# Loading feed-forward weights in fp32 through one hardware queue, with the casts on GpSimd, in a fused scan and feed-forward kernel

## The chip, the core and the metric

The kernel runs on one core of a Trainium2 chip. The metric is the device time of one execution in microseconds. A core has TensorE (PE in the profile, with its weight loads as PEld), VectorE (DVE), ScalarE (ACT), GpSimd (POOL) and SyncE (SP), and 16 DMA engines that move data between HBM and the on-chip SBUF. Matmuls write into PSUM, [...]. Each engine runs its own instructions in order, and semaphores tie the engines together.

## The reference

The first half is a chunked linear recurrence over 4 batches, 8 heads and 768 time steps, with head dimension 32 and state dimension 16. Its result, as 3072 tokens of 256 features, goes through a feed-forward layer with a squared ReLU.

```python
cum = np.cumsum(la, axis=-1)                       # la = log of the decay a
L = np.exp(cum[..., :, None] - cum[..., None, :]) * causal
y_intra = ((Cc @ Bc^T) * L) @ xc
y_inter = (Cc @ state) * np.exp(cum)[..., None]
state   = decay_full * state + sum_j decay_from_j * Bc_j xc_j^T
...
h   = np.maximum(x @ w_in, 0.0)                    # (3072, 256) @ (256, 2048)
out = h * h @ w_out                                # (3072, 2048) @ (2048, 256)
```

All inputs and the output are fp32; w_in and w_out are 2 MB each.

## The kernel before, in words

The work is cut into twelve units: batch b of 4 and a stretch of 256 time steps j of 3. Unit k is batch k % 4, stretch k // 4 (`UNITS`). Partition t of a unit holds two neighbouring time steps. The decays are carried by a cumulative product of a (`P_sb` and its reciprocal `Pinv`), with which C and B are scaled.

What happens to a unit: `ph_load` (L124) loads C, B and x in fp32. `prep_c` (L164), `prep_b` (L172) and `prep_x` (L183) scale and cast them to bf16 into `jt` and `xs`. `ph_tr` (L202) transposes `jt` into `bct`, on PE for the first five units and with a DMA transpose for the others. `ph_mt` (L234) makes the score matrices in PSUM banks 0 to 3; `ph_mask` (L256) applies the causal mask on DVE and writes them as bf16 `mts`, either straight from PSUM or from a bf16 copy `raw` that `ph_raw` (L251) made on ACT. `ph_yu` (L263) makes the outputs y of a unit ("Y") from `mts`, `xs` and the carried state `Sd`, copied into `T`, and the state products U of a unit ("U") from `xs` and `jt`. `ph_s` (L336) folds U into the state z, and GpSimd spreads z into the bf16 operand `Sd` (L357).

The feed-forward part of unit b has eight steps fp of 256 hidden features. `mm1` (L371, in the schedule "u") multiplies T by w_in, and ACT applies the ReLU (L380); `square` (L383, "s") squares on DVE; `mm2` (L389, "d") multiplies by w_out and accumulates. In the schedule u13 is mm1 of unit 1 at step 3.

The order is written by hand. Up to the word `first` (L542) it is the plain sequence of calls; `first` then lists the steps of units 0 and 1, with the third unit's preparation, masks and products between them; after it a table by step number (`at`) drives units 2 to 11, one mm1 and one mm2 per step. PE passes the list strictly in order.

The weights are in bf16 in SBUF, in four tiles for each matrix. `load_w_in` (L149) and `load_w_out` (L153) are DMAs issued by GpSimd that cast from fp32 on the way. They stand between GpSimd's other instructions: w_in block 0 before the first unit is prepared, then w_out 0 in two parts, w_in 1, w_out 1, w_in 2, then the third unit (C and B in fp32, x cast on the way by `load_x`, L141), then w_out 2, w_in 3, w_out 3. Two tiny casts into `spare` (L452, L508) hold GpSimd back until a result of another engine is there. The second one, with three one-element memsets into the load buffers (L131), holds the loads of units 3 to 5 back until a mask of the third unit is done. The other loads are issued by SyncE.

Of the kernel before, what the change touches and what calls it, by code (L numbers as in the profile page):

```python
# [10 lines left out]
FP32 = mybir.dt.float32  # L11
BF16 = mybir.dt.bfloat16
# [11 lines left out]
def _dap(base: bass.AP, offset_elems: int, dims):  # L24

    return bass.AP(tensor=base.tensor, offset=base.offset + offset_elems,
                   ap=[list(d) for d in dims])
# [3 lines left out]
def kernel(  # L31
# [15 lines left out]
    NU = 12  # L47
# [36 lines left out]
    pick_p = const.tile([96, 2, 12], FP32, name="pick_p")  # L84
    P_sb = const.tile([128, 2, 96], FP32, name="P_sb")
    Pinv = const.tile([128, 2, 96], FP32, name="Pinv")
    spare = const.tile([128, 1], FP32, name="spare")
    Ptot = const.tile([128, 2, 12], FP32, name="Ptot")


# [1 line left out]

    idle = const.tile([128, 128], BF16, name="idle")

    w_in_b = [wpool.tile([128, 2, 512], BF16, name=f"w_in_b{i}") for i in range(4)]
    w_out_b = [wpool.tile([128, 4, 256], BF16, name=f"w_out_b{i}") for i in range(4)]
    QP = const.tile([128, 12, 2, 4], FP32, name="QP")

    pp = psum.tile([128, 8, 512], FP32, name="pp")
# [21 lines left out]

    loaded, live = {}, {}

    def ph_load(k, order="CBx", eng=None, gate=False):  # L124
        b, j = UNITS[k]
        t = loaded.setdefault(k, {})
        for what in order:
            src, w = {"B": (B, N), "C": (C, N), "x": (x, D)}[what]
            dst = nat.tile([128, NH, 2 * w], FP32, tag=f"{what}_nat", name=f"{what}_nat{k}")
            if gate:  # L130
                nc.gpsimd.memset(dst[:, 0, 0:1], 0.0)  # L131
            parts = 2 if k == NU - 1 and what == "B" else 1
            for p in range(parts):
                hs = NH // parts
                (eng or nc.sync).dma_start(  # L135
                    out=dst[:, p * hs:(p + 1) * hs],
                    in_=_dap(src, (b * NH * S + p * hs * S + j * 256) * w,
                             [[2 * w, 128], [S * w, hs], [1, 2 * w]]))
            t[what] = dst

    def load_x(k):  # L141

        b, j = UNITS[k]
        xs = const.tile([128, NH, 2 * D], BF16, name=f"xb{k}")
        nc.gpsimd.dma_start(out=xs, in_=_dap(x, (b * NH * S + j * 256) * D,
                                             [[2 * D, 128], [S * D, NH], [1, 2 * D]]))
        live.setdefault(k, {})["xs"] = xs

    def load_w_in(i):  # L149
        nc.gpsimd.dma_start(  # L150
            out=w_in_b[i], in_=_dap(moe_w_in, i * 512, [[2048, 128], [128 * 2048, 2], [1, 512]]))

    def load_w_out(i, parts=1):  # L153
        n = 4 // parts
        for p in range(parts):
            nc.gpsimd.dma_start(  # L156
                out=w_out_b[i][:, p * n:(p + 1) * n],
                in_=_dap(moe_w_out, (i * 4 + p * n) * 128 * 256, [[256, 128], [128 * 256, n], [1, 256]]))

    def idle_products(n):  # L160
        for _ in range(n):
# [10 lines left out]
    def prep_b(k, eng):  # L172
        b, j = UNITS[k]
        for g in range(2):
            o = _fap(jt[k % 3], 16 * g, [[384, 2], [32, 4], [1, 16]])
            i = _fap(loaded[k]["B"], 128 * g, [[16, 2], [32, 4], [1, 16]])
            if k == 0:
                eng.copy(out=o, in_=i)
            else:
                eng.tensor_tensor(out=o, in0=i, in1=_fap(Pinv, b * 24 + 12 * g + j, [[96, 2], [3, 4], [0, 16]]),  # L180
                                  op=ALU.mult)

    def prep_x(k, eng):  # L183

        xs = prep.tile([128, NH, 2 * D], BF16, tag="xs", name=f"xs{k}")
        if k == 0:
            eng.tensor_tensor(
                out=_fap(xs, 0, [[64, 8], [32, 2], [1, 32]]),
                in0=_fap(loaded[k]["x"], 0, [[64, 8], [32, 2], [1, 32]]),
                in1=_fap(Pinv, 0, [[3, 8], [96, 2], [0, 32]]), op=ALU.mult)  # L190
        else:
            eng.tensor_copy(out=xs, in_=loaded[k]["x"])  # L192
        live.setdefault(k, {})["xs"] = xs
# [62 lines left out]
    def ph_mask(k, q):  # L256
        t = raw_scores.pop((k, q), None)
        nc.vector.tensor_tensor(  # L258
            out=live[k]["mts"][:, q],
            in0=(pp[:, q, :] if t is None else t).rearrange("p (r g i) -> p r g i", r=2, g=2),  # L260
            in1=_fap(mask, 0, [[128, 2], [0, 2], [1, 128]]), op=ALU.mult)
# [108 lines left out]

    def mm1(blk, fp, edge):  # L371
        h = bank(edge)
        wb, wo = fp // 2, 2 * (fp % 2)
        for i in range(2):
            for g in range(2):
                nc.tensor.matmul(pp[:, h, i * 256:(i + 1) * 256], w_in_b[wb][:, g, (wo + i) * 128:(wo + i + 1) * 128],  # L376
                                 T[blk][:, g].rearrange("p r u t -> p (r u t)"),
                                 start=(g == 0), stop=(g == 1), skip_group_check=True)
        hb = fpool.tile([128, 2, 256], BF16, tag="hb", name=f"hb{blk}_{fp}")
        nc.scalar.activation(out=hb.rearrange("p i t -> p (i t)"), in_=pp[:, h, :], func=AF.Relu)  # L380
        hbs[(blk, fp)] = hb
# [6 lines left out]

    def mm2(blk, fp):  # L389
        h2 = h2s.pop((blk, fp))  # L390
        wb, wo = fp // 2, 2 * (fp % 2)
        end = blk == NU - 1
        for r, i in [(r, i) for r in range(2) for i in range(2)] if end else [(r, i) for i in range(2) for r in range(2)]:
            f = 2 * fp + i
            o = pp[:, r, 0:256] if end else pp[:, 7 if blk else 6, r * 256:(r + 1) * 256]
            nc.tensor.matmul(o, h2[:, i, r * 128:(r + 1) * 128], w_out_b[wb][:, wo + i, :],  # L396
                             start=(f == 0 and (end or r == 0)), stop=(f == 15), skip_group_check=True)
        if fp < 7:
            return
        b, j = UNITS[blk]  # L400
        o = (b * S + j * 256) * 256
        osb = opool.tile([128, 512], FP32, tag="osb", name=f"osb{blk}")
        if end:
            nc.vector.tensor_copy(out=osb[:, 0:256], in_=pp[:, 0, 0:256])
            nc.scalar.copy(out=osb[:, 256:512], in_=pp[:, 1, 0:256])
            for r, eng in enumerate((nc.sync, nc.scalar)):
                eng.dma_start(out=_dap(out, o + r * 256, [[512, 128], [1, 256]]), in_=osb[:, r * 256:(r + 1) * 256])
        else:
            nc.scalar.copy(out=osb, in_=pp[:, 7 if blk else 6, :])  # L409
            nc.sync.dma_start(out=_dap(out, o, [[512, 128], [1, 512]]), in_=osb)  # L410

    with tc.manual_schedule():
# [2 lines left out]
        ph_load(0, "B", nc.scalar)  # L415
        nc.scalar.dma_start(out=cf, in_=cf_d.ap())
        ph_load(0, "x")
        ph_load(1)

        def keep(t, pattern, base, step, op=ALU.is_ge, fill=0.0):  # L420

# [27 lines left out]
        for r in range(2):  # L449
            nc.tensor.transpose(ptr[:, r, :], _fap(cp_r, r, [[2, 128]]), eye_f)  # L450
        nc.scalar.copy(out=P_sb, in_=ptr)
        nc.gpsimd.tensor_copy(out=spare, in_=P_sb[:, 0, 0:1])  # L452
        load_w_in(0)
        idle_products(NIDLE[1])
        prep_b(0, nc.scalar)
        prep_c(0, nc.vector)
# [7 lines left out]
            out=_fap(QP, 0, [[8, 12], [4, 2], [1, 4]]), in0=_fap(Ptot, 0, [[1, 12], [12, 2], [0, 4]]),  # L464
            in1=_fap(quad, 0, [[0, 12], [0, 2], [1, 4]]), op=ALU.mult)
        prep_c(1, nc.gpsimd)
        load_w_out(0, 2)
        load_w_in(1)
        idle_products(NIDLE[2])
        later = []  # L470
        ph_mt(0)
# [3 lines left out]
        ph_s(0, 0)  # L475
        U01 = const.tile([128, 64], FP32, name="U01")
        nc.scalar.copy(out=U01, in_=pp[:, 7, 384:448])
        prep_b(1, nc.vector)
        prep_x(1, nc.gpsimd)
        load_w_out(1)  # L480
        idle_products(NIDLE[3])
        ph_tr(1)
        idle_products(NIDLE[4])
        for q in range(1, 4):
            ph_mask(0, q)
        ph_mt(1)
        ph_raw(1, 3)
        for q in range(4):
            ph_mask(1, q)
        ph_yu(y=0, late=True, h=(4, 5))  # L490
        ph_yu(u=1)
        ph_s(1, 0)
        load_w_in(2)
        ph_load(2, "CB", nc.gpsimd)
        load_x(2)
        load_w_out(2)
        load_w_in(3)
        load_w_out(3)
        order[:] = [4, 5]

        def release():
            for fn in later:
                fn()
            later.clear()
            prep_c(2, nc.gpsimd)

        def later_loads():
            nc.gpsimd.tensor_copy(out=spare, in_=live[2]["mts"][:, 0, 0, 0, 0:1])  # L508
            for k in (3, 4, 5):
                ph_load(k, gate=k == 3)  # L510

        def third_state():
            ph_yu(u=2, h=(4, 5))
# [14 lines left out]
        def scores_only():  # L528
            order[:] = [h for h in order if h > 3]

        phases = {
            "z1b": lambda: (ph_s(1, 1, later=later), ph_s(0, 1, later=later, raw=U01)), "Y1": second_outputs, "load": release, "free": scores_only,
            "inv": lambda: nc.vector.reciprocal(out=_fap(Pinv, 1, [[96, 2], [3, 32], [1, 2]]),
                                                in_=_fap(P_sb, 1, [[96, 2], [3, 32], [1, 2]])),
# [3 lines left out]
        for q in range(4):  # L538
# [1 line left out]


        first = """  # L542
            u00 u01 s00 Y1 d00 s01 u10 z1b d01 u11 load s10 u02 s11 u03 d10 inv s02 u12 d11 s03 u13 d02 s12 d03 u04
            s13 d12 u05 B2 s04 d13 free tr2 u14 s05 u15 d04 s14 mt2 d05 m20 load3 s15 U2 m21 d14 m22 prep3 d15 u06 m23
            u16 lend s06 u07 s16 Y2 d06 u17 s07 d16 d07 s17""".split()
        for what in first:
# [88 lines left out]
```

## Time and profile before

The median of three executions is 116.9 us (116.67 to 117.16). The profiled execution spans 116.2 us.

| | busy us | share of the span | instructions |
|---|---|---|---|
| PE matmuls | 108.1 | 93% | 1650 |
| PE weight loads | 91.3 | 79% | 1650 |
| VectorE | 82.0 | 71% | 183 |
| ScalarE | 74.7 | 64% | 136 |
| GpSimd | 51.5 | 44% | 103 |

The granted TensorE clock is full throughout. The DMA engines are busy from about 2 to 24 us and again from 27 to 60 us. The DMA queue of SyncE moves 10.13 MB in 40736 packets, that of GpSimd 2.49 MB in 4352 packets; HBM is read for 10.64 MB and written for 3.15 MB. An issue of a w_in block takes 6.3 us to land in the median, of a whole w_out block 7.5 us.

A busy share is a mean over very different stages, and GpSimd's 44% contains issues of DMAs (L150, L156, L135, L145 on POOL), which occupy it for 0.7 to 0.9 us each. The groups give the cost of one instruction, the timeline and the chain of waits tell when it counted. A name such as `w_out_b<-h` in the profile is output from input, with buffer numbers left out.

### The profile page before, as it was taken

How to read it: one execution, taken by the hardware profiler on the slowest of the kernel's cores; microseconds unless marked ns; L12 is line 12 of the kernel's file. 1: busy time of each engine (PE TensorE's matmuls, PEld its weight loads, DVE VectorE, ACT ScalarE, POOL GpSimd, SP SyncE). 2: the span in 40 equal slices, each digit the busy share in tenths (PEclk: the TensorE clock that was granted, in tenths of full speed). 3: DMA queues.
4: the chain of work that ended last, by engine and by line, in shares of the span. 5: the costliest groups of instructions: out<-in, count | busy, mean ns of one | idle time of the engine just before them, and what ended most of it. 6: DMA issues, size and time to landing. Idle time of an engine off the chain costs nothing.

```text
span 116.2 us, 4018 instructions
## 1 busy us (share of the span) xinstructions
PE 108.1 (93%) x1650; PEld 91.3 (79%) x1650; DVE 82.0 (71%) x183; ACT 74.7 (64%) x136; POOL 51.5 (44%) x103
## 2 busy tenths in 40 slices
PE   6897899789999999989999999999999999999980
PEld 6875578658767888868888888889888888888860
DVE  4599969749389898968849958757677578345440
ACT  3345665616767686675676776677767766966830
POOL 7589999123779826959309319037020020000000
PEclk9999999999999999999999999999999999999999
DMA  3999999945999369989908728532050020020202
GB/s 70 203 169 155 113 152 182 180 63 98 189 183 250 78 99 179 235 106 238 195 13 192 146 72 156 117 116 49 0 156 11 0 93 8 13 77 0 90 6 90
DMA packets 46403, 13.20 MB, mean 114 GB/s; under 512 B 41392, under 2 KB 44912, under 8 KB 46384
## 3 DMA queue, kind: packets, MB, share of 16 engines
q1 hardware_dynamic: 40736, 10.13, 46.3%
q0 software_dynamic: 4352, 2.49, 17.4%
q10 hardware_dynamic: 1296, 0.32, 1.2%
q8 instruction: 13, 0.21, 0.8%
q14 instruction: 6, 0.05, 0.2%
HBM read 10.64 MB, written 3.15 MB: 119 GB/s over the span
## 4 chain that ended last, share of the span: by engine, by line
PE 64%; DMA 15%; POOL 12%; ACT 2%; issue 2%; SPq 1%; DVE 1%; POOLq 0%
PE pp L396 28%; PE pp L376 26%; DMA w_out_b<-in_moe_w_out_dram 6%; DMA bct<-jt 5%; DMA x_nat<-in_x_dram 4%; PE pp L273 4%; PE pp L162 3%; POOL Sd L357 3%; PE pp L240 3%; POOL w_out_b L156 1%; POOL jt L167 1%; POOL xs L192 1%; POOL w_in_b L150 1%; SPq L135 1%; POOL jt L180 1%
## 5 line engine op out<-in xcount | busy, mean ns | idle before, releaser
L380 ACT ACTIVATE hb<-pp 128x512 bf16<-128x512 f32 x96 | 56.6, 597 | 26.7 <-PE pp L376 25.8
L396 PE MATMUL pp<-w_out_b,h 128*128 128x256 bf16 x384 | 56.5, 273 | 1.2 <-DMA w_out_b<-in_moe_w_out_dram 1.2
L376 PE MATMUL pp<-T,w_in_b 128*128 128x256 bf16 x384 | 56.6, 273 | 0.4 <-ACT T L333 0.2
L386 DVE TENSOR_TENSOR h<-hb 128x512 bf16<-128x512 bf16 x96 | 43.3, 457 | 17.3 <-ACT hb L380 17.0
L396 PEld LDWEIGHTS <-h 128*128 128x128 bf16 x384 | 37.1, 98 | 6.2 <-issue 1.5
L376 PEld LDWEIGHTS <-w_in_b 128*128 128x128 bf16 x384 | 36.5, 98 | 6.8 <-issue 1.8
L258 DVE TENSOR_TENSOR mts<-pp,mask 128x512 bf16<-128x512 f32 x46 | 30.9, 681 | 2.1 <-PE pp L240 2.0
L357 POOL TENSOR_TENSOR Sd<-z,QP 128x256 bf16<-128x256 f32 x20 | 12.5, 635 | 30.3 <-DVE z L352 29.7
L167 POOL TENSOR_TENSOR jt<-C_nat,P_sb 128x128 bf16<-128x128 f32 x22 | 10.4, 491 | 3.8 <-PE pp L273 2.0
L180 POOL TENSOR_TENSOR jt<-B_nat,Pinv 128x128 bf16<-128x128 f32 x18 | 8.9, 512 | 0.6 <-DMA B_nat<-in_B_dram 0.6
L352 DVE SCALAR_TENSOR_TENSOR z<-z,Ptot,pp 128x64 f32<-128x64 f32 x14 | 3.9, 280 | 5.6 <-ACT T L333 5.0
L192 POOL CAST xs<-x_nat 128x512 bf16<-128x512 f32 x10 | 7.4, 740 | 0.6 <-DMA x_nat<-in_x_dram 0.6
L162 PE MATMUL pp<-idle 128*128 128x128 bf16 x72 | 6.5, 262 | 1.1 <-DVE idle L425 1.1
L162 PEld LDWEIGHTS <-idle 128*128 128x128 bf16 x72 | 5.8, 123 | 1.1 <-DVE idle L425 1.1
L333 ACT CAST T<-pp 128x512 bf16<-128x512 f32 x10 | 5.9, 586 | 1.2 <-PE pp L273 0.6
L409 ACT COPY osb<-pp 128x512 f32<-128x512 f32 x11 | 6.4, 583 | 0.2 <-PE pp L396 0.2
L240 PE MATMUL pp<-bct 32*64 32x256 bf16 x192 | 5.1, 280 | 1.1 <-DMA bct<-jt 0.5
L273 PE MATMUL pp<-mts,xs 64*32 64x128 bf16 x352 | 5.4, 219 | 0.1
L273 PE MATMUL pp<-bct,Sd 128*128 128x128 bf16 x40 | 4.2, 220 | 0.1
L273 PEld LDWEIGHTS <-xs 64*32 64x32 bf16 x352 | 3.7, 90 | 0.8 <-issue 0.6
L240 PEld LDWEIGHTS <-bct 32*64 32x64 bf16 x192 | 2.0, 102 | 2.5 <-DMA bct<-jt 0.6
L156 POOL DMA_DIRECT2D w_out_b<-in_moe_w_out_dram x5 | 3.9, 782 | 0.0
(65 smaller groups left out, 43.5 us busy)
## 6 DMA issues: line engine op xcount, KB each, us to landing
x_nat<-in_x_dram SPq DMA_DIRECT2D x11, 256.0 KB, 4.6
out_dram<-osb SPq DMA_DIRECT2D x11, 256.0 KB, 2.3
C_nat<-in_C_dram SPq DMA_DIRECT2D x11, 128.0 KB, 3.9
B_nat<-in_B_dram SPq DMA_DIRECT2D x9, 128.0 KB, 4.2
w_in_b<-in_moe_w_in_dram POOLq DMA_DIRECT2D x4, 256.0 KB, 6.3
w_out_b<-in_moe_w_out_dram POOLq DMA_DIRECT2D x3, 256.0 KB, 7.5
w_out_b<-in_moe_w_out_dram POOLq DMA_DIRECT2D x2, 128.0 KB, 3.7
B_nat<-in_B_dram ACTq DMA_DIRECT2D x1, 128.0 KB, 3.3
```

The source lines that it names most:

```text
L162: nc.tensor.matmul(pp[:, 5, 0:128], idle, idle, start=True, stop=True, skip_group_check=True)
L167: eng.tensor_tensor(out=_fap(jt[k % 3], 128 + 144 * g, [[384, 2], [32, 4], [1, 16]]), in0=_fap(loaded[k]["C"], 128 * g, [[16, 2], [32, 4], ...
L180: eng.tensor_tensor(out=o, in0=i, in1=_fap(Pinv, b * 24 + 12 * g + j, [[96, 2], [3, 4], [0, 16]]), op=ALU.mult)
L192: eng.tensor_copy(out=xs, in_=loaded[k]["x"])
L240: nc.tensor.matmul(pp[64 * u:64 * u + 64, q, r * 256:r * 256 + 256], bct[32 * q:32 * q + 32, r, 0, u * 64:u * 64 + 64], _fap(bct[32 * q:32 ...
L258: nc.vector.tensor_tensor(out=live[k]["mts"][:, q], in0=(pp[:, q, :] if t is None else t).rearrange("p (r g i) -> p r g i", r=2, g=2), in1 ...
L273: nc.tensor.matmul(dst, w, v, start=bool(need), stop=False, skip_group_check=True, **({} if pos is None else {"tile_position": pos}))
L357: nc.gpsimd.tensor_tensor(out=_fap(S_d, 0, [[128, 2], [32, 4], [1, 32]]), in0=_fap(z, 0, [[32, 2], [0, 4], [1, 32]]), in1=_fap(QP, ((b * 3 ...
L376: nc.tensor.matmul(pp[:, h, i * 256:(i + 1) * 256], w_in_b[wb][:, g, (wo + i) * 128:(wo + i + 1) * 128], T[blk][:, g].rearrange("p r u t - ...
L380: nc.scalar.activation(out=hb.rearrange("p i t -> p (i t)"), in_=pp[:, h, :], func=AF.Relu)
L386: nc.vector.tensor_tensor(out=h2, in0=hb, in1=hb, op=ALU.mult)
L396: nc.tensor.matmul(o, h2[:, i, r * 128:(r + 1) * 128], w_out_b[wb][:, wo + i, :], start=(f == 0 and (end or r == 0)), stop=(f == 15), skip ...
```

## The change

All weights are now loaded in fp32 by SyncE's queue, in one fixed order together with the loads of units 0 to 3, and GpSimd casts them to bf16 in halves (`cast_w_in`, `cast_w_out`), so that each of the eight steps has a tile of its own. A w_out load now takes rows 4p to 4p+3 of a block of 512 into partition p, so that a packet can hold up to four rows. Because a step's hidden features are then spread with a step of four, the cast of w_in picks every fourth column to match. The third unit is loaded in fp32 by the same queue, and its x is cast by GpSimd. The gates are gone. Bank 2 of the first unit's scores is copied by ScalarE like bank 3, the order of some steps at the start changes (Y of unit 0 before the scores of unit 1, U of unit 1 after u00), and the loads of the last units are split. The aim is to have the weights arrive in a known order, without GpSimd spending its time on issues.

```diff
+    w_in_f = [wpool.tile([128, 2, 512], FP32, name=f"w_in_f{i}") for i in range(4)]
+    w_out_f = [wpool.tile([128, 4, 256], FP32, name=f"w_out_f{i}") for i in range(4)]
+    w_in_b = [wpool.tile([128, 2, 2, 128], BF16, name=f"w_in_b{i}") for i in range(8)]
+    w_out_b = [wpool.tile([128, 2, 256], BF16, name=f"w_out_b{i}") for i in range(8)]
...
-            parts = 2 if k == NU - 1 and what == "B" else 1
+            parts = 2 if k == NU - 1 or (k == NU - 2 and what == "x") else 1
...
+    def load_w_in(i):
+        nc.sync.dma_start(out=w_in_f[i], in_=_dap(moe_w_in, i * 512, [[2048, 128], [128 * 2048, 2], [1, 512]]))
+    def load_w_out(i):
+        n = 2 if i < 2 else 4
+        for f in range(0, 4, n):
+            nc.sync.dma_start(out=w_out_f[i][:, f:f + n],
+                              in_=_dap(moe_w_out, (i * 512 + f) * 256, [[1024, 128], [256, n], [1, 256]]))
+    def cast_w_in(i):
+        for e in range(2):
+            nc.gpsimd.tensor_copy(out=w_in_b[2 * i + e],
+                                  in_=_fap(w_in_f[i], 2 * e, [[512, 2], [1, 2], [4, 128]]))
+    def cast_w_out(i):
+        for e in range(2):
+            nc.gpsimd.tensor_copy(out=w_out_b[2 * i + e], in_=w_out_f[i][:, 2 * e:2 * e + 2])
...
-        ph_load(1)
+        ph_load(1, "CB")
+        load_w_in(0)
+        ph_load(1, "x")
+        load_w_out(0)
+        load_w_in(1)
+        load_w_out(1)
+        load_w_in(2)
+        ph_load(2, "CB")
+        load_w_out(2)
+        load_w_in(3)
+        ph_load(2, "x")
+        load_w_out(3)
+        ph_load(3)
...
+        ph_raw(0, 2)
         prep_b(1, nc.vector)
+        cast_w_in(0)
         prep_x(1, nc.gpsimd)
...
-        for q in range(1, 4):
+        for q in (1, 3, 2):
             ph_mask(0, q)
+        ph_yu(y=0, late=True, h=(4, 5))
         ph_mt(1)
...
-        ph_yu(y=0, late=True, h=(4, 5))
-        ph_yu(u=1)
-        ph_s(1, 0)
...
         def release():
+            prep_c(2, nc.gpsimd)
+            cast_w_out(2)
+            cast_w_in(3)
             for fn in later:
                 fn()
             later.clear()
-            prep_c(2, nc.gpsimd)
+            prep_x(2, nc.gpsimd)
+            cast_w_out(3)
         def later_loads():
-            nc.gpsimd.tensor_copy(out=spare, in_=live[2]["mts"][:, 0, 0, 0, 0:1])
-            for k in (3, 4, 5):
-                ph_load(k, gate=k == 3)
+            ph_load(4)
+            ph_load(5)
+        def second_state():
+            ph_yu(u=1)
+            ph_s(1, 0)
+            cast_w_out(0)
+            cast_w_in(1)
+            cast_w_out(1)
+            cast_w_in(2)
...
-            u00 u01 s00 Y1 d00 s01 u10 z1b d01 u11 load s10 u02 s11 u03 d10 inv s02 u12 d11 s03 u13 d02 s12 d03 u04
+            u00 U1 u01 s00 Y1 d00 s01 u10 z1b d01 u11 load s10 u02 s11 u03 d10 inv s02 u12 d11 s03 u13 d02 s12 d03 u04
```

## The prediction

> **What bounds the kernel now.** I read the chain of work first, because a mean over the span mixes a start-up and a steady part. It is dense TensorE (PE) work from 23.78 us on; the largest wait in it comes just before (columns: start, us, what).
>
> ```profile
> 13.57 0.91 POOL C_nat L135
> 14.48 0.89 POOL B_nat L135
> 15.38 0.84 POOL xb L145
> 16.22 7.52 DMA w_out_b<-in_moe_w_out_dram
> 23.78 0.60 PE pp L396 x4
> ```
>
> GpSimd (POOL) issues the third unit's loads one by one, then the third w_out block, whose landing releases PE. The timeline of PE around it:
>
> ```profile
> 23.78 0.60 PE L396 MATMUL pp<-w_out_b,h 128*128 128x256 bf16 x4 [1.18 <-DMA w_out_b<-in_moe_w_out_dram]
> ...
> 25.21 0.25 PE L273 MATMUL pp<-xb,jt 64*32 64x64 bf16 x16
> ...
> 31.11 0.51 PE L225 MATMUL pp<-eye_b,jt 128*128 128x128 bf16 x6
> ...
> 37.55 0.61 PE L376 MATMUL pp<-T,w_in_b 128*128 128x256 bf16 x4
> ```
>
> So PE loses 1.18 us at d04, reaches the third unit's state products ("U2", from xb) at 25.21, the fourth unit's transposes at 31.11 and the regular schedule at 37.55. From there the windows show PE 14.31 of 14.80 us busy up to 52.3: what is gained or lost before 37.55 moves the end, what is hidden behind PE later does not. The waits, by engine (total, times, longest), say what else held PE or fed it:
>
> ```profile
> ACT z L350 <- PE pp L273: 2.2, 1, 2.2
> POOL jt L167 <- PE pp L273: 2.0, 1, 2.0
> PE pp L396 <- DMA w_out_b<-in_moe_w_out_dram: 1.2, 1, 1.2
> PEld L376 <- DMA w_in_b<-in_moe_w_in_dram: 0.4, 1, 0.4
> PEld L225 <- POOL jt L180: 0.3, 1, 0.3
> ```
>
> The last line is the wait before 31.11: POOL prepares the fourth unit late, since its loads leave at 25.91 (gated) and its C is first used at 28.56.
>
> The price list for POOL, from the groups by shape and the tiles (ns min/median/max in the second):
>
> ```profile
> L357 POOL TENSOR_TENSOR Sd<-z,QP 128x256 bf16<-128x256 f32 x7 | 4.5, 652 | 0.6 <-ACT z L350 0.6
> L156 POOL DMA_DIRECT2D w_out_b<-in_moe_w_out_dram x4 | 3.1, 788 | 0.0
> L192 POOL CAST xs<-x_nat x10: 606/802/807, 10.9 to 79.9; 128x512 bf16<-128x512 f32 x10
> L386 DVE TENSOR_TENSOR h<-hb x96: 354/426/829, 13.2 to 111.4; 128x512 bf16<-128x512 bf16 x96
> ```
>
> A 512-element cast is 0.61 us alone and 0.80 us beside VectorE (DVE) squares.
>
> [...]
>
> **The change, part by part.**
>
> *Removed from POOL:* twelve DMA issues of 0.72 to 0.92 us, about 9.8 us, and the gates (two 0.31 us casts, three 0.09 us memsets). The window 9 to 16 (busy us and instructions of PE, PEld, DVE, ACT, POOL; clock, DMA share, GB/s) has POOL full, mostly with them:
>
> ```profile
> 9.00:16.00 7.00, 5.84 (x138) 3.99 (x136) 5.95 (x13) 4.32 (x9) 6.96 (x10) 1.00 1.08 132
> ```
>
> *Landing of the weights.* B of unit 1 lands at 8.1 (its reader on DVE starts then). Then, in queue order: a 512 KB block at the 347 GB/s of the window 36 to 37 (2 KB output packets) takes 1.5 us; B, C and x at the 190 GB/s of 2 to 7 take 0.7, 0.7 and 1.4. So w_in0 lands at 9.6, x1 11.0, w_out0 12.5, w_in1 14.0, w_out1 15.5, w_in2 17.0, C2 and B2 18.4, w_out2 19.9 (before 23.74), w_in3 21.4, x2 22.8, w_out3 24.3, unit 3 27.0. Units 4 and 5 follow ungated, so prep3 no longer waits for data. Four w_out rows make longer packets; at this rate I give that nothing, since landing then isn't the last wait.
>
> *Casts on POOL, new:* sixteen of 512 elements. The eight of w_out are contiguous, like the xs cast: 0.61 to 0.80; I take 0.70, as the Sd rows, too, stand some 8% over their 606 ns. The eight of w_in read one element in four (step 16 bytes). [...] I take 1.10. Also new is the xs cast of unit 2 (0.75), which a casting DMA did.
>
> *POOL's order after* is fixed by the program: Sd0, w_in0 casts, xs1, Sd1, w_out0, w_in1, w_out1, w_in2, prep_c2, w_out2, w_in3, two Sd, xs2, w_out3, Sd2, prep3. Casts of w_in0: 9.6 to 11.8; xs1 to 12.4; PE's U1, ACT's z and Sd1 to 13.2–13.3. Then six casts of each kind up to xs2: 6 x 0.70 + 6 x 1.10 = 10.8; prep_c2 0.88, two Sd 1.45, xs2 0.75, sum 3.1 (rows of before at 19.94, 18.44, 46.21). **xs2 is ready at 13.2 + 10.8 + 3.1 = 27.1.** U2 has to wait for it, and everything behind U2 on PE (d14, d15, u06, u16, u07, Y2) waits too; PE is in order.
>
> *PE up to U2.* Sd0 no longer stands behind DMA issues (10.93 before, 8.8 now), so Y0 isn't held by it. But mt1 moves behind Y0, hence the four masks of unit 1 some 0.1 to 0.5 us later (Y1 at 13.2 before). The w_in wait of 0.4 goes, the d04 wait of 1.18 goes. PE would be at U2 at about 25.2 - 1.2 + 0.2 = 24.2. The casts that u02 to d05 need end earlier: fp 2 of w_in at 15.7 (needed 15.7), fp 4 about 19.3 (20.1), w_out fp 5 about 22.7 (23.6). So one stall of 2.9, at 27.1: **1.9 later than before.**
>
> *After U2.* Sd2 follows the w_out3 casts (28.5) to 29.2, Y2 arrives at 27.1 + 2.4 = 29.5. prep3 runs at once: C 30.1, B 31.1, while PE arrives at tr3 at 27.1 + 5.9 - 0.3 = 32.7. So the 0.3 of the line above goes, and 0.15 of small waits for squares and drains: -0.45.
>
> *At nothing:* raw copy of bank 2 on ScalarE, 0.59 us in the idle 0.95 before the bct copy (L228); its mask reads bf16. Split loads of the last units lie under dense PE. Steady part: the same instructions.
>
> Sum: 116.9 + 1.9 - 0.45 = 118.35, say **118.4**.
>
> **Rivals.**
> - *Faster: no stride penalty.* If w_in casts cost 0.61 to 0.70 as well, POOL is ready for w_in3 about its landing at 21.4, and xs2 comes at 21.4 + 1.3 + 1.3 + 0.65 = 24.65. U2 is 0.55 early, tr3 gains 0.45, some casts end ahead of their reader: 116.9 - 1.1 = 115.8. For it: nothing in the trace shows strided reads as dearer. [...]
> - [...]
> - *Much slower.* Casts 1.5 and 0.75 [...]: 13.2 + 13.5 + 3.1 = 29.8, +4.6 - 0.45: 121.0. [...]
>
> **How the numbers follow.** Chances: forecast 0.38, faster 0.36, same 0.13, much slower 0.13. The forecast's own spread (w_in cast 1.05 to 1.2) is 117.6 to 119.5, so above 117.5 lies 0.49, below 116.3 0.37, between 0.14. The range 115.6 to 120.4 leaves out the worst of the slow case and the best of the fast one.
>
> **What would show it.** The groups should have the w_in cast near 1.1 us and the w_out cast near 0.7; the waits a line of PE or its weight load for POOL xs (L191) of 2 to 3 us near 24 to 27; no wait for a weights DMA after 12 us. A w_in cast under 0.8 makes the forecast wrong and the fast rival right. Weights that land over a microsecond later than listed, or DVE squares over 0.6 us, make the slow one right.

## The result, and the profile after

The changed kernel takes 122.06 us in the median (121.83 to 122.86), beside 117.03 us for the kernel before on the same chip: a ratio of 1.0447, interval 1.0391 to 1.0502. The forecast was 118.4 with a range up to 120.4. The direction was right, the size was not: 5.0 us were lost where 1.45 were forecast.

I read the chain of work that ended last first, as for the kernel before (start, us, what; from 4.71 us on):

```profile
4.71 1.16 SPq L142
5.91 5.93 DMA x_nat<-in_x_dram
11.86 2.25 SPq L135
14.16 3.39 SPq L147
17.59 7.40 DMA w_in_f<-in_moe_w_in_dram
25.05 2.55 POOL w_in_b L152 x2
27.60 1.33 POOL Sd L356 x2
28.92 0.76 POOL xs L191
29.98 0.98 PE pp L393 x8
```

Before, the chain was on PE from 23.78 us on. Now it runs through SyncE's issues and one weight block until 25.05, then through GpSimd (POOL): the two casts of w_in block 3, two spreads of z into Sd, the cast of the third unit's x. Only at 29.98 does it reach PE. (L135 is `ph_load`, L142 and L147 are the issues of w_in and w_out.) The timeline of PE shows where it stood still:

```profile
12.07 0.61 PE L374 MATMUL pp<-T,w_in_b 128*128 128x256 bf16 x4 [1.10 <-POOL w_in_b L152]
13.86 0.25 PE L272 MATMUL pp<-xs,jt 64*32 64x64 bf16 x16 [1.18 <-POOL xs L191]
...
29.73 0.26 PE L272 MATMUL pp<-xs,jt 64*32 64x64 bf16 x16 [1.84 <-POOL xs L191]
...
35.50 0.50 PE L224 MATMUL pp<-eye_b,jt 128*128 128x128 bf16 x6
...
41.91 0.61 PE L374 MATMUL pp<-T,w_in_b 128*128 128x256 bf16 x4
```

The line at 29.73 is U2, the third unit's state products, the one at 35.50 the fourth unit's transposes, the one at 41.91 the start of the regular schedule. The wait of 1.84 us for xs is the one that the prediction named; without it PE would have been at U2 at 27.9 (29.73 - 1.84), itself 4 us later than in the trace of `before_again`. Ahead of it stand two that it did not have: PE waits 1.10 us for the first weight casts and 1.18 us for the x of unit 1, at 11 to 14 us. From 41.91 to the end of the span are 78.3 us; in the kernel before (the trace of `before_again`, below) 78.4. So the whole loss lies ahead of the regular schedule.

The price list of GpSimd, from the groups by shape (busy us, mean ns, idle before):

```profile
L152 POOL CAST w_in_b<-w_in_f 128x512 bf16<-128x512 f32 x8 | 9.4, 1195 | 2.1 <-DMA w_in_f<-in_moe_w_in_dram 2.1
L157 POOL CAST w_out_b<-w_out_f 128x512 bf16<-128x512 f32 x8 | 5.3, 684 | 0.0
```

1.195 and 0.684 us, where 1.10 and 0.70 were put down. And GpSimd's timeline at its two ends:

```profile
10.93 2.13 POOL L152 CAST w_in_b<-w_in_f 128x512 bf16<-128x512 f32 x2 [1.79 <-DMA w_in_f<-in_moe_w_in_dram]
13.01 0.80 POOL L191 CAST xs<-x_nat 128x512 bf16<-128x512 f32 x1
14.48 0.61 POOL L356 TENSOR_TENSOR Sd<-z,QP 128x256 bf16<-128x256 f32 x1 [0.67 <-ACT z L349]
...
25.05 2.55 POOL L152 CAST w_in_b<-w_in_f 128x512 bf16<-128x512 f32 x2 [0.35 <-DMA w_in_f<-in_moe_w_in_dram]
27.57 1.36 POOL L356 TENSOR_TENSOR Sd<-z,QP 128x256 bf16<-128x256 f32 x2
28.87 0.80 POOL L191 CAST xs<-x_nat 128x512 bf16<-128x512 f32 x1
```

The first block of w_in landed at 10.93 (9.6 in the prediction's list), and Sd1 ended at 15.09 instead of 13.2. From there GpSimd is full, but for 0.35 us, until xs2 is ready at 29.67. (Neighbouring rows of this view overlap by some 0.05 us.)

The windows show two side effects (us, busy us and instructions of PE, PEld, DVE, ACT, POOL; clock, DMA share, GB/s):

```profile
10.00:14.00 4.00, 1.72 (x68) 1.02 (x67) 2.98 (x5) 1.74 (x4) 2.88 (x3) 1.00 1.06 326
14.00:18.00 4.00, 3.60 (x66) 2.31 (x53) 2.13 (x5) 1.49 (x4) 3.52 (x5) 0.72 1.07 289
18.00:22.00 4.00, 3.83 (x30) 2.94 (x28) 2.63 (x4) 2.35 (x5) 4.00 (x5) 0.85 0.68 200
```

After four microseconds in which PE worked for 1.72, its granted clock falls to 0.72 and 0.85 of full speed; and from 18 to 22 us the DMA engines carry 200 GB/s at a share of 0.68, though weights are still to come.

### The profile page after: what moved, and what is told of

Its sections match the earlier page's. It is cut to its first block, busy times and chain, and to the rows that moved or that the text cites. A ratio compares the mean times of both kernels' runs of the same rounds, so it can differ in the third digit from the quotient of the medians.

```text
span 120.2 us, 4034 instructions
## 1 busy us (share of the span) xinstructions
PE 110.3 (92%) x1650; PEld 92.6 (77%) x1650; DVE 85.4 (71%) x183; ACT 75.0 (62%) x137; POOL 56.7 (47%) x103
## 4 chain that ended last, share of the span: by engine, by line
PE 56%; DMA 19%; SPq 10%; POOL 8%; issue 1%; DVE 1%; ACT 1%; POOLq 0%
PE pp L393 26%; PE pp L374 24%; DMA x_nat<-in_x_dram 9%; DMA w_in_f<-in_moe_w_in_dram 6%; SPq L135 6%; PE pp L272 4%; DMA bct<-jt 4%; SPq L147 3%; POOL Sd L356 2%; PE pp L239 2%; POOL w_in_b L152 2%; POOL xs L191 2%; SPq L142 1%; POOL jt L179 1%; POOL jt L166 1%
## 5 line engine op out<-in xcount | busy, mean ns | idle before, releaser
L384 DVE TENSOR_TENSOR h<-hb 128x512 bf16<-128x512 bf16 x96 | 46.9, 497 | 18.0 <-ACT hb L378 17.8
L374 PE MATMUL pp<-T,w_in_b 128*128 128x256 bf16 x384 | 57.5, 276 | 1.1 <-POOL w_in_b L152 1.1
L393 PE MATMUL pp<-w_out_b,h 128*128 128x256 bf16 x384 | 57.5, 276 | 0.6 <-DVE h L384 0.4
L374 PEld LDWEIGHTS <-w_in_b 128*128 128x128 bf16 x384 | 37.0, 99 | 7.9 <-issue 1.8
L257 DVE TENSOR_TENSOR mts<-pp,mask 128x512 bf16<-128x512 f32 x45 | 30.4, 682 | 1.5 <-PE pp L239 1.3
L356 POOL TENSOR_TENSOR Sd<-z,QP 128x256 bf16<-128x256 f32 x20 | 12.5, 635 | 33.4 <-DVE z L351 29.2
L152 POOL CAST w_in_b<-w_in_f 128x512 bf16<-128x512 f32 x8 | 9.4, 1195 | 2.1 <-DMA w_in_f<-in_moe_w_in_dram 2.1
L191 POOL CAST xs<-x_nat 128x512 bf16<-128x512 f32 x11 | 8.5, 770 | 0.3 <-DMA x_nat<-in_x_dram 0.3
L272 PE MATMUL pp<-xs,jt 64*32 64x64 bf16 x160 | 3.0, 195 | 3.1 <-POOL xs L191 3.0
L272 PEld LDWEIGHTS <-jt 64*32 64x32 bf16 x160 | 1.9, 89 | 4.7 <-issue 3.6
L157 POOL CAST w_out_b<-w_out_f 128x512 bf16<-128x512 f32 x8 | 5.3, 684 | 0.0
```

Of the source, the lines that this page charges most:

```text
L152: nc.gpsimd.tensor_copy(out=w_in_b[2 * i + e], in_=_fap(w_in_f[i], 2 * e, [[512, 2], [1, 2], [4, 128]]))
L257: nc.vector.tensor_tensor(out=live[k]["mts"][:, q], in0=(pp[:, q, :] if t is None else t).rearrange("p (r g i) -> p r g i", r=2, g=2), in1 ...
L272: nc.tensor.matmul(dst, w, v, start=bool(need), stop=False, skip_group_check=True, **({} if pos is None else {"tile_position": pos}))
L356: nc.gpsimd.tensor_tensor(out=_fap(S_d, 0, [[128, 2], [32, 4], [1, 32]]), in0=_fap(z, 0, [[32, 2], [0, 4], [1, 32]]), in1=_fap(QP, ((b * 3 ...
L374: nc.tensor.matmul(pp[:, h, i * 256:(i + 1) * 256], w_in_b[fp][:, g, i, :], T[blk][:, g].rearrange("p r u t -> p (r u t)"), start=(g == 0) ...
L384: nc.vector.tensor_tensor(out=h2, in0=hb, in1=hb, op=ALU.mult)
```

## The experiments

The starting theory (A): GpSimd's chain to xs2 (casts, then the two Sd, then the x cast) sets U2, as predicted, and started later than predicted. Rivals: the landing of the weights sets U2 (B); PE's lower clock does (C); the order at the start costs time by itself (D); the base of the forecast was off (E). GpSimd's timeline and PE's are read in each run. Runs on different occasions have their own runs of the kernel before beside them, so ratios are compared.

### The kernel before, again

No edit. The profiled execution that the prediction rests on spans 116.2 us and took 117.93, a microsecond more than the median of 116.9. (In the runs here the time is 1.7 to 1.9 us more than the span.)

> The kernel before, unchanged, for a second trace. Theory E (the profiled execution of before, 117.93 us, was an untypically long one, and the 1.18 us wait for w_out at 23.8 us belongs to it): this trace spans about 115 us, has that wait under 0.3 us and reaches the regular schedule near 36.4 us instead of 37.55. Otherwise the wait is there again and the span is 116.

Measured: 116.59 us, ratio 1.0001 (0.9977 to 1.0024), span 114.7. From its timeline of PE, the d04 group, U2, the fourth unit's transposes and the regular schedule:

```profile
23.38 0.61 PE L396 MATMUL pp<-w_out_b,h 128*128 128x256 bf16 x4
23.92 0.25 PE L273 MATMUL pp<-xb,jt 64*32 64x64 bf16 x16
...
29.83 0.51 PE L225 MATMUL pp<-eye_b,jt 128*128 128x128 bf16 x6
...
36.31 0.61 PE L376 MATMUL pp<-T,w_in_b 128*128 128x256 bf16 x4
```

No wait for a weights DMA at d04. The 1.18 us that the prediction took off was in one long execution, and is not in this one, whose 116.38 us lie near the median. Against this trace the change delays U2 by 29.73 - 23.92 = 5.8 us and the regular schedule by 41.91 - 36.31 = 5.6.

### The changed kernel, again

No edit; a second trace of the changed kernel, and a base for the runs below.

> The changed kernel, unchanged, beside the others on one chip. 121.5 to 122.2 us; U2 waits for xs2 by 1 to 2 us again, the TensorE clock drops again between 14 and 20 us. If the first w_in block lands 0.4 us earlier than in its first trace, as in the runs so far, the time is at the lower end.

Measured: 121.54 us, ratio 1.0413 (1.0368 to 1.0458). w_in 0 landed at 11.35, xs2 was ready at 29.63, the regular schedule began at 42.08. U2 in the timeline of PE:

```profile
29.68 0.25 PE L272 MATMUL pp<-xs,jt 64*32 64x64 bf16 x16 [0.51 <-POOL xs L191]
```

The wait for xs2 is 0.51 us, not the 1 to 2 that were expected. U2 stands where it did, but here PE is late too: it would have been there at 29.17. Two late paths meet at U2, GpSimd's and PE's own, and xs2 comes last, by 1.8 us in one trace and by 0.5 in the other.

### The third unit's x ahead of w_in 3

```diff
         load_w_out(2)
-        load_w_in(3)
         ph_load(2, "x")
+        load_w_in(3)
...
             cast_w_out(2)
+            prep_x(2, nc.gpsimd)
             cast_w_in(3)
-            for fn in later:
-                fn()
-            later.clear()
-            prep_x(2, nc.gpsimd)
-            cast_w_out(3)
```

The w_out 3 casts and the two Sd (`later`) follow the third unit's own Sd instead.

> The changed kernel with the third unit's x loaded ahead of w_in block 3 and cast ahead of the w_in 3 casts; the w_out 3 casts and the two Sd of units 0 and 1 move behind the third unit's Sd. All work is kept. Theory A (GpSimd's queue up to the xs2 cast holds U2): xs2 is ready near 25.5 us instead of 29.67, TensorE meets U2 without a wait near 27.9, the end comes 1.8 us earlier, about 120.2. Theory B (the loads land late in SyncE's one queue): x2 is late as well, U2 still waits, gain under 0.5. Theory C (the TensorE clock dropped after idling at 11 to 14 us): no change, because the drop comes before.

Measured: 120.59 us, ratio 1.0338 (1.0285 to 1.0391). xs2 was ready at 24.71 and U2 no longer waited:

```profile
27.95 0.25 PE L272 MATMUL pp<-xs,jt 64*32 64x64 bf16 x16
```

So the wait is gone, but U2 came only 1.8 us earlier, since PE itself arrives late, and the regular schedule began at 40.61, 1.3 to 1.5 earlier. Of that, 0.4 is no gain of the edit: w_in 0, ahead of everything that was edited, landed at 10.49 in this trace (10.93 in the changed kernel's first). PE's weight loads waited for squares 7 times, 2.7 us in all (1.5 in the changed kernel), and GpSimd has no gap from 14.4 to 27.1. The theory holds for the wait; the gain is about 1 us, a fifth of the loss, and the intervals of the two ratios (1.0413 and 1.0338) just overlap.

### The casts without the stride

```diff
-                              in_=_dap(moe_w_out, (i * 512 + f) * 256, [[1024, 128], [256, n], [1, 256]]))
+                              in_=_dap(moe_w_out, (i * 4 + f) * 128 * 256, [[256, 128], [128 * 256, n], [1, 256]]))
...
-                                  in_=_fap(w_in_f[i], 2 * e, [[512, 2], [1, 2], [4, 128]]))
+                                  in_=_fap(w_in_f[i], 256 * e, [[512, 2], [128, 2], [1, 128]]))
```

> The changed kernel with w_out rows loaded as before (row p of each 128 to partition p) and so w_in cast from adjacent columns. All work is kept. Theory A with the step of 16 bytes as its cause: a w_in cast takes 0.65 us instead of 1.20, Sd1 comes 0.9 earlier; without a later wait xs2 would be ready 4.0 earlier. Theory B: w_in 3 still lands near 25 us, GpSimd waits for it some 3 us, and U2 comes only about 1.2 earlier, the time 0.5 to 1.3 lower (about 121). If the step costs nothing, the cast stays at 1.2 and the time at 122.

Measured: 120.63 us, ratio 1.0326 (1.0247 to 1.0404). The groups, and U2 in the timeline of PE:

```profile
L152 POOL CAST w_in_b<-w_in_f 128x512 bf16<-128x512 f32 x8 | 5.1, 671 | 4.2 <-DMA w_in_f<-in_moe_w_in_dram 4.1
```

```profile
27.94 0.26 PE L272 MATMUL pp<-xs,jt 64*32 64x64 bf16 x16 [2.75 <-POOL xs L191]
```

A step of 16 bytes costs 1.195 - 0.671 = 0.52 us on 512 elements. The faster casts don't help much, though: GpSimd now waits 4.1 us for w_in blocks, 2.19 of them for w_in 3, which lands at 24.74. PE would have been at U2 at 25.19 and waits 2.75 us there. Behind the slow casts stood the landing of w_in 3, as one theory said, and xs2 is queued behind its casts.

### Both

The two edits together.

> e1 and e2 together: adjacent columns, and the third unit's x loaded and cast ahead of w_in 3. All work is kept. Theory A and B: with both of the last waits before U2 gone, TensorE reaches U2 near 25.2 without a wait and is next held by u06, whose w_in 3 block lands near 25.5 and is cast by 26.2; the time falls by 2 us or more against e1 and e2, to 118.5 or less. If something else sets U2, the time stays near 120.6.

> The same kernel as e6_plain_and_x2_first (both edits: w_out rows laid out as before with casts from neighbouring columns, and the third unit's x loaded and cast ahead of w_in 3), once more, for a trace of it. Theory F (the loss of the change is the sum of three: slow casts, the place of the third unit's x in queue and on GpSimd, and the order at the start): w_in casts at 0.6 to 0.75 us, U2 without a wait for xs and at about 25, the regular schedule (step 22) at about 37.5, as in b2_start_order (37.48), time 117.8 to 118.3, ratio about 1.01. Rival G (something else remains, such as casts that hold up VectorE's squares, or weights that land late): step 22 later than 38.3, and waits of PE for squares or weights of over 1.5 us between U1 and step 22.

Measured: ratio 1.0113 (1.0050 to 1.0175), and in the repetition 118.69 us, 1.0132 (1.0058 to 1.0207). The first profile fell on an execution of 373 us, so the second is read, in its timeline of PE:

```profile
14.63 0.60 PE L393 MATMUL pp<-w_out_b,h 128*128 128x256 bf16 x4
...
25.09 0.25 PE L272 MATMUL pp<-xs,jt 64*32 64x64 bf16 x16
```

Each edit alone took 0.8 to 0.9% off, both take about 3%: with slow casts GpSimd is late anyway, with fast casts and x last it waits for w_in 3, and only with both is xs2 (23.45) ready before PE comes (25.1). The granted clock is 1.00 in each of the windows from 10 to 26 us. U2 is 1.2 us later than in the kernel before, the regular schedule (38.10) 1.8 later. Of that, 0.93 is there at 14.63, the first mm2 (d00; 13.70 in `before_again`), after waits of PE for masks of unit 1 as in the run on the start order below. The expectation of 37.5 was missed by 0.6, so the sum of three parts that it assumed is not quite the whole.

### A warm PE

```diff
             ph_mask(1, q)
+        idle_products(14)
         order[:] = [4, 5]
...
         def second_state():
+            idle_products(14)
             ph_yu(u=1)
```

Fourteen idle products each (matmuls whose result nobody reads) fill the two gaps of PE at 11 to 14 us.

> The changed kernel with 14 idle products (results not used) before u00 and 14 before the state products of unit 1, to fill TensorE's two idle stretches between 11 and 14 us. Theory C: the granted clock stays full in 14 to 20 us, and the time falls by 1.5 to 2 us. Theory A: the clock stays full too, but TensorE only waits longer for xs2 at U2: no change within 0.3 us.

Measured: 120.87 us, ratio 1.0374 (1.0320 to 1.0429), granted clock 0.997. The gain of 0.4% lies within the intervals and is too small for the clock to be the cause of the loss; w_in 0 landed 0.35 us earlier in this trace, and PE still waited 1.16 us at U2 for xs2:

```profile
28.71 0.25 PE L272 MATMUL pp<-xs,jt 64*32 64x64 bf16 x16 [1.16 <-POOL xs L191]
```

With a fast PE the wait for GpSimd and the waits for squares (PE 1.4, its weight loads 2.6 us) take the gain back.

### The order at the start, on the kernel before

```diff
+        ph_raw(0, 2)
         prep_b(1, nc.vector)
...
-        for q in range(1, 4):
+        for q in (1, 3, 2):
             ph_mask(0, q)
+        ph_yu(y=0, late=True, h=(4, 5))
         ph_mt(1)
...
-            u00 u01 s00
+            u00 U1 u01 s00
```

Loads and casts stay as before; U of unit 1, with the issues behind it, moves behind u00.

> The kernel before with the start order of the changed one alone: Y of unit 0 before the scores of unit 1, U of unit 1 after u00 with the loads behind it, bank 2 of unit 0 copied by ScalarE, masks 1, 3, 2. All work is kept. Theory A and B: this part isn't the cause, the time stays within 0.6 us of 117.0 (the GpSimd loads behind U1 leave perhaps 0.3 later). Theory D (the order of the start is what costs): 1.5 us or more slower.

Measured: 117.74 us, ratio 1.0088 (1.0054 to 1.0121): 1.0 us slower. Its Y of unit 1 ends at about 15.1 (13.8 in `before_again`), its regular schedule begins at 37.48 (36.31): PE waits three times, 1.1 us in all, for masks of units 0 and 1 (waits by engine: total, times, longest):

```profile
PE pp L273 <- DVE mts L258: 1.1, 3, 0.5
```

The prediction gave the same edits 0.1 to 0.5 us, and 0.2 in its sum. The three parts of it (raw copy, Y of unit 0 ahead, U of unit 1 behind u00) were not taken apart.

### All three parts undone

```diff
-        ph_load(1, "CB")
-        load_w_in(0)
-        ph_load(1, "x")
+        ph_load(1)
+        load_w_in(0)
...
-        ph_raw(0, 2)
         prep_b(1, nc.vector)
-        cast_w_in(0)
         prep_x(1, nc.gpsimd)
+        cast_w_in(0)
```

And the order of masks, Y of unit 0 and U of unit 1 as in the kernel before. What is left of the change are fp32 weights in SyncE's queue and plain casts.

> Both edits of e6 and in addition the order at the start as in the kernel before: x of unit 1 ahead of w_in 0 in the queue, xs of unit 1 ahead of the w_in 0 casts, no raw copy of bank 2, masks 1, 2, 3 and then the scores of unit 1, Y of unit 0 after the masks of unit 1, U of unit 1 ahead of u00. All weights still come in fp32 through SyncE's queue and are cast by GpSimd. Theory F: another 0.7 to 1.1 us less than e6_again, step 22 at 36.3 to 36.7, time 116.6 to 117.2, within 0.5% of the kernel before: then the three parts hold the whole loss. Rival G: not below 117.5; w_in 0 lands 0.7 us later in the queue, u00 waits for its casts and gives the gain back.

Measured: 118.39 us, ratio 1.0142 (1.0100 to 1.0185), no better than with the new start order. From the timeline of PE:

```profile
12.49 0.61 PE L374 MATMUL pp<-T,w_in_b 128*128 128x256 bf16 x4 [1.23 <-POOL w_in_b L152]
```

w_in 0, now behind x of unit 1, lands at 11.82, and u00 waits 1.23 us for its casts. So d00 comes at 14.69, as in the repetition above (14.63). The new order at the start loses a microsecond by itself, and bridges a wait of that length: undoing it exchanges one for the other. The theory of three adding parts falls here; the rival named this.

### The first block as before

```diff
-        load_w_in(0)
...
+        nc.gpsimd.tensor_copy(out=spare, in_=P_sb[:, 0, 0:1])
+        for e in range(2):
+            nc.gpsimd.dma_start(out=w_in_b[e], in_=_dap(moe_w_in, e * 256, [[2048, 128], [128 * 2048, 2], [1, 256]]))
...
-        cast_w_in(0)
```

On top of the last kernel.

> e9_all_three, with w_in block 0 alone loaded as in the kernel before: by casting DMAs that GpSimd issues at 5.4 us (two halves, about 1.6 us of issue), ahead of any other work of GpSimd; the other three blocks of w_in and all of w_out stay in fp32 in SyncE's queue with casts on GpSimd. Theory J (what e6 and e9 still lose is where the first w_in block comes in SyncE's queue: it landed at 10.3 to 11.8, while before had it by 11.9 without a cast behind it): u00 near 11.9 without a wait for POOL, d00 at about 13.7 (e9 14.7), U2 at 23.9 to 24.3, step 22 at 36.4 to 37.2 (the fourth unit's transposes may wait up to 0.7 for GpSimd, which w_in 3 holds up), time 116.9 to 117.6. Rival K (the loss sits in VectorE's squares beside the casts, or in the later blocks): d00 early but U2 not before 24.7, time 118 or more.

Measured: ratio 1.0101 (1.0066 to 1.0136). The regular schedule began at 37.29, U2 was at 24.66; d00 was at 14.66 and not at 13.7. The timeline of PE says why:

```profile
9.38 0.51 PE L225 MATMUL pp<-eye_b,jt 128*128 128x128 bf16 x6 [0.68 <-DVE jt L180]
...
13.65 0.61 PE L375 MATMUL pp<-T,w_in_b 128*128 128x256 bf16 x4 [0.58 <-DMA w_in_b<-in_moe_w_in_dram]
```

Two waits come ahead of d00. The first, for the prepared B of unit 1, isn't a landing. VectorE's two instructions for it took 1.09 us together, where the kernel before has 0.49, and the second (698 ns, 292 there) ran beside GpSimd's spread of z; first the two engines here, then the kernel before:

```profile
8.23 1.09 DVE L180 TENSOR_TENSOR jt<-B_nat,Pinv 128x128 bf16<-128x128 f32 x2
8.51 0.67 POOL L357 TENSOR_TENSOR Sd<-z,QP 128x256 bf16<-128x256 f32 x1
...
8.11 0.49 DVE L180 TENSOR_TENSOR jt<-B_nat,Pinv 128x128 bf16<-128x128 f32 x2
```

There the spread started at 10.29, behind issues of DMAs. So the run brought a cost of its own. The second wait is for w_in 0: its second half is there only at 13.6, though it was issued by 7.44 (6.54 for the whole block in the kernel before, which had it by 11.95). The second issue explains 0.9 us of that. The rest fits the other loads that are now in flight at the same time: w_out 0 and w_in 1 are issued at 5.85 to 7.6, where the kernel before issued nothing of them before 8.09. That load of the DMA engines was not varied by itself, so this remains a reading.

### The longer packets by themselves

The repetition above (both edits), but with four w_out rows to a partition as in the change, contiguous casts, and the stride in the weight loads of mm1:

```diff
-                nc.tensor.matmul(pp[:, h, i * 256:(i + 1) * 256], w_in_b[fp][:, g, i, :],
+                nc.tensor.matmul(pp[:, h, i * 256:(i + 1) * 256], _fap(w_in_b[fp // 2], 512 * g + 2 * (fp % 2) + i, [[4, 128]]),
```

> As e6_again, but the change's layout of w_out (four rows to a partition) is kept; GpSimd casts w_in from neighbouring columns, and the weight loads of mm1 on PE pick every fourth column instead. Tells what the longer packets are worth once the slow cast is gone. Theory F: casts at 0.6 to 0.75, weight loads of mm1 no longer than before (they overlap the matmuls), so the time is that of e6_again within 0.4 us. Rival H (longer packets land sooner): w_in 3 and w_out 3 land 1 us or more earlier than in e6_again and the time is 0.5 us or more below it. Rival I (strided weight loads slow PE): mm1 groups take longer than the 0.44 us a product pair of e6_again, in all twelve units, and the time is over 119.

Measured: 118.28 us, ratio 1.0144 (1.0064 to 1.0224); the same as without. w_in 3 lands at 25.08 (25.23 without). A strided weight load takes 113 ns and not 98 in the median, and the matmuls stay at 273. The longer packets (2 and 4 KB in the trace's DMA records, which have size, start and duration of every packet, where the other layout has 1 KB) bring nothing measurable here. The stride brings no measurable loss on PE, and 0.52 us a cast on GpSimd.

### C and B of the third unit out of SyncE's queue

Two attempts to find why w_in 3 lands at 25 and not at 21.4. The first, on the kernel with plain casts, lets ScalarE issue them:

```diff
-        ph_load(2, "CB")
...
         ph_raw(1, 3)
+        ph_load(2, "CB", nc.scalar)
```

> The kernel with adjacent columns (e2), and C and B of the third unit issued by ScalarE's queue after its raw copy of unit 1 instead of in the middle of SyncE's. All work is kept. Theory B (SyncE's queue is blocked at issue behind the small packets of C2 and B2, 3.3 us at the w_out 2 issue): the w_out 2 and w_in 3 issues take under 1 us each, w_in 3 lands near 22 instead of 24.7, xs2 is ready near 25.5 instead of 27.9, and the time falls by about 2 us against e2, to 118.5. Rival: the DMA engines' rate is the limit, w_in 3 still lands after 24 us and the time stays within 0.5 us of e2's 120.6.

Measured: 125.18 us, ratio 1.0754 (1.0680 to 1.0827). From the waits by engine:

```profile
ACT hb L378 <- DMA w_in_f<-in_moe_w_in_dram: 5.9, 1, 5.9
PE pp L272 <- POOL Sd L356: 5.5, 1, 5.5
```

ScalarE's two issues left only at 15.30 and 17.41, and held up its ReLU and with it Sd and PE for 5.5 us, so the time tells nothing of the question. The queue does: SyncE's issue of w_in 3 left at 12.53 (17.84 in the kernel with plain casts), it took at most 7.9 us to land, that is by 21.1, and the DMA engines carried 375 and 324 GB/s from 16 to 20 us (shown below).

The second builds on the kernel with the first block as before, and lets GpSimd issue them in front of its casts of w_out 0:

```diff
             ph_s(1, 0)
+            ph_load(2, "CB", nc.gpsimd)
             cast_w_out(0)
```

> e10 and, in addition, C and B of the third unit issued by GpSimd in front of its casts of w_out 0 (two issues of about 0.9 us), so that after unit 1 SyncE's queue holds only weights and x until w_out 3. Tells why w_in 3 lands at 25 instead of 21.4. Theory L (SyncE's issues are held back behind the 512-byte packets of C2 and B2: issues of 3 to 4 us there): SyncE's issue of w_in 3 done before 14, w_in 3 landed by 22, no wait of GpSimd for w_in 3, transposes of the fourth unit without a wait, step 22 at 36.3 to 36.8, time 116.5 to 117.2. Rival M (the DMA engines' bandwidth decides): w_in 3 lands at 23.5 or later all the same, and the time is that of e10 or, for the 1.8 us of issues on GpSimd, above it.

Measured: 120.72 us, ratio 1.0312 (1.0221 to 1.0403). In the timeline of SyncE's queue, the issue of w_in 3:

```profile
12.37 4.36 SPq L143 DMA_DIRECT2D w_in_f<-in_moe_w_in_dram x1
```

It takes 4.36 us without C2 and B2 in that queue, and w_in 3 lands at 24.6, although the DMA engines have a share of 1.00 to 1.16 all the while. So the theory that the short packets of C2 and B2 in SyncE's own queue hold its issues back falls as it was put. The time is that of two issues more ahead of the w_out 0 casts: PE waits 0.91 us for them at 15.6, and its clock drops to 0.50 from 16 to 18 us. What the rival M forecast (w_in 3 at 23.5 or later all the same, the time above the run before) came out. (The 512-byte packets that the expectation names for C2 and B2 are of 128 bytes in SyncE's queue in the changed kernel, by the DMA records.) The two runs also differ in what is ahead of w_in 3. With ScalarE as the issuer, C2 and B2 left at 15.30 and 17.41 and x2 came behind w_in 3. With GpSimd, x2 is ahead of w_in 3, and C2 and B2 left at 13.12 and 14.06, while SyncE stood at w_in 3. The windows, first with ScalarE, then with GpSimd:

```profile
16.00:18.00 2.00, 0.00 (x0) 0.00 (x0) 0.00 (x0) 0.17 (x1) 0.00 (x0) 0.78 1.08 375
18.00:20.00 2.00, 0.43 (x3) 0.28 (x4) 0.58 (x2) 1.30 (x4) 1.39 (x3) 0.50 1.15 324
...
18.00:20.00 2.00, 1.96 (x14) 1.36 (x12) 1.83 (x2) 1.01 (x3) 1.69 (x4) 0.79 1.16 193
```

From 18 to 20 us the engines are as busy in both, but carry 324 GB/s in the one and 193 in the other, where by the DMA records x2 (packets of 256 bytes), C2 and B2 take three quarters of their time. That fits M: what w_in 3 waits for there is the time of the engines, whichever queue the loads came from. It is a reading, since the order was not varied by itself, and it does not cover the changed kernel, where the engines are not full from 18 to 22 us (share 0.68); why w_in 3 is late there stays open.

No version here beats the kernel before.

## Why the prediction was wrong

**The mechanism was right, by a small margin.** "U2 has to wait for it" is what the page shows: PE waits 1.84 us for xs L191, the two w_in casts, two Sd and the x cast are the last steps of the chain, and moving x ahead takes the wait away. But the forecast was a wait of 2.9, with PE ready at 24.2; in the changed kernel's second trace it is 0.51, with PE ready at 29.17.

**The cast prices were nearly right.** w_in 1.195 (1.10), w_out 0.684 (0.70), xs 0.77 (0.75). The 1.10 was the author's estimate and not shown: the trace of before has no such cast on GpSimd. The plain-column run measured what the step costs, 0.52 us in the mean (1.195 and 0.671), with casts beside VectorE's work in both, and 0.48 between the shortest casts (1.087 and 0.608). The six casts of each kind up to xs2 took 11.3 us in the timeline (10.8), `prep_c(2)` 1.14 (0.88); with 0.35 of waiting for w_in 3 the chain from Sd1 to xs2 took 14.6 us, not 13.9. That term was 0.7 too small.

**"Casts of w_in0: 9.6 to 11.8 ... Sd1 to 13.2–13.3" failed.** This is the start of the chain, and it was 1.85 us late: 1.33 from w_in 0, which landed at 10.93, and 0.5 from the hop over PE and ScalarE (xs1 ready at 13.81, Sd1 at 15.09: 1.3 us, not 0.8). The landing list gives each load the engines for itself, in the order of the queue: 1.5 us at 347 GB/s for w_in 0. The trace shows otherwise. By its DMA records the last packet of C and B of unit 1 ended at 7.09; from there to 10.93 the engines carried 267 GB/s, or 1.0 MB, of which w_in 0 is 0.52. The other half is x of unit 1 and weights, which stand behind w_in 0 in the queue. Alone at that rate the block would have taken 2.0 us (an estimate), not 3.8. The list also begins late, by luck on the side that makes the miss smaller: it has B of unit 1 land at 8.1 because its reader starts then, but in the trace of before VectorE worked on a mask until 8.09 and didn't wait for B, and the last 128-byte packet of C and B ended at 7.07. The 1.85 and the 0.7 of the chain make xs2 late by 2.6 us: 29.67, not 27.1. In the changed kernel's second trace w_in 0 landed at 11.35 and xs2 was ready at 29.63.

**The base failed.** The prediction took "the d04 wait of 1.18" off PE's way, and measured U2 from 25.21. Both belong to a profiled execution a microsecond above the median; in the second trace of before U2 is at 23.92 without that wait. The forecast was added to the median all the same. In terms of the sum: 2.6 for U2 by a late xs2, 1.3 for the base (25.21 - 23.92), and 0.25 for what is regained after U2 (0.2, not 0.45) are 4.15, which is the miss between these two traces (5.6 - 1.45); between the medians it is 3.6.

**The start order was costed at 0.1 to 0.5 and measures 1.0** on the kernel before. In the changed kernel it covers part of the wait for w_in 0, so the two don't add.

**"PE would be at U2 at 24.2" failed too**: it was ready at 27.9. The two gaps at 11 to 14 us and the clock after them are in no part of the prediction. They cost little beyond the wait at U2, which hides them, as the warm run shows, and they became visible when x was moved ahead, and in the second trace, where PE was ready only at 29.2.

**"No wait for a weights DMA after 12 us" failed**: w_in 3 landed at 25.0, not 21.4. In the changed kernel that is 0.35 us of waiting, in the kernel with plain casts 2.2. This also undoes the faster rival, which had xs2 at 24.65 with casts at 0.65: measured with such casts, xs2 came at 27.88 and the kernel lost 3.3%.

**"Much slower" had nearly the right numbers** (xs2 29.8, 121.0 us) for another reason: casts of 1.5 and 0.75 us, which did not occur. Of its signs one did: weights that land over a microsecond later than listed (w_in 3 at 25.05, not 21.4). Squares took 497 ns in the mean (459 in `before_again`), under the 0.6 us of its other sign; whether the casts slow them was not shown, since no run separates it.

Undone together, slow casts and the place of x account for some 3 of the 4 to 4.5%; the last 1.0 to 1.4% stay in all four versions with both undone (both edits, the longer packets, all three parts undone, the first block as before; the last run adds two issues on GpSimd). Half or more of it is lost by d00, which comes at 14.6 to 14.8 us there (13.70 before), but PE stands still ahead of it for different things: for masks with both edits, for the casts of w_in 0 with all three parts undone, for B of unit 1 and then w_in 0 with the first block as before. Later w_in 3, near 25 us, also shows on PE in one of them: with all three parts undone GpSimd is so late behind it that the fourth unit's transposes wait 0.64 us for a prepared B. Whether one cause, such as the load on the DMA engines, stands behind these is not shown.

## What to carry to other kernels

Before a wait is subtracted, see whether the profiled execution is a median one: if its span is above the others' by as much as the wait, the wait isn't there to be gained (here 117.93 beside a median of 116.9, and a wait of 1.18 us). When casts move to an in-order engine, write its list from the landing of its first input, and price that landing with all the traffic that is in flight then, loads issued behind it included (here 3.8 us for w_in 0, where 1.5 was listed); what stands last in the list (here a 0.8 us cast that a whole unit waits for) should stand ahead of bulk work with slack. Two causes in series on one chain hide each other: undone alone each brought a fifth of the loss, together they brought two thirds.

## What else the runs showed

SyncE's own issues took 0.4 to 1.2 us each up to 8 us, but 3.4 us (L147 at 14.16) and 4.0 us (L135 at 21.03) in the changed kernel, and 4.36 us in `e11_and_cb2_by_gpsimd`, once several weight blocks were on their way; what is behind the two in the changed kernel's queue left at 17.59 (w_in 3) and 25.09 (x of the fourth unit). ScalarE, too, stood still for 5.9 us in `e5_cb2_on_act`, with its two issues in that stretch.

PE's clock fell to 0.50 at 16 to 19 us in the changed kernel after 10 to 14 us with 1.72 of 4.00 us busy; with 2.22 (x ahead alone) it fell too (0.63 in the mean of 14 to 18 us), with 2.53 (all three parts undone) and 2.96 (both edits) it stayed at 1.00, in one trace each. In the warm run, where idle products fill the two gaps (1.10 and 1.18 us in the changed kernel), the granted clock was 0.997 in the mean of the span, beside 0.986.
